# DMA in strict turns from the fourth pair on: a pair's loads, its transposes, then the next pair's loads, held back on POOL

## The chip, the core and the metric

One core of one Trainium2 chip runs the kernel. The metric is the device time of one execution in microseconds (us). The profile of one execution is a little shorter than its device time: 207.6 us of span against 209.35 us for the kernel before. Lower is better. The engines are named as in the profile: PE is TensorE's matmuls, PEld its weight loads, DVE is VectorE, ACT is ScalarE, POOL is GpSimd, SP is SyncE (here it only issues DMAs). L381 is line 381 of that kernel's file; the same line of code has another number in another version.

## The reference

Retention attention with a decaying state per head, then a dense layer with `h * cos(h)` between its two matmuls.

```python
# q, k, v: (4, 8, 768, 64); w_in: (512, 2048); w_out: (2048, 512)
for t in range(S):
    state = gamma * state + outer(k[t], v[t])      # per batch and head
    y[t] = scale * q[t] @ state
x = y.transpose(0, 2, 1, 3).reshape(3072, 512)
h = x @ w_in
out = (h * cos(h)) @ w_out
```

## The kernel before

The sequence is cut into 12 "pairs": pair `p` is one chunk of 128 positions of two batches. For each pair q, k and v are loaded (six loads of 256 KB), from pair 3 on q and v are scaled and converted to bf16 by POOL and k is converted by ACT (the first pairs are shared out otherwise), q and k are transposed (by PE for pairs 0 to 3, by DMA from pair 4 on), and PE computes scores (`stage_a`), outputs and state (`stage_y`). Two pairs give a group of 512 tokens; each group goes through the dense layer. The attention of later pairs is interleaved with the dense layer of earlier groups.

All work of an engine is done in the program's order (in the trace after the change ACT sat idle for 1.8 us at a k conversion, up to 76.1 us, while outputs finished by 72.2 us stood behind it). The program uses seven work banks of 128x512 in PSUM, the memory that matmuls write to; a matmul into a bank must wait until DVE or ACT has read the bank's old content (once for 2.7 us, in the same trace). ACT does both the k conversions, which wait for loads, and the evictions of banks, for which PE waits.

```python
NB = 3                                       # buffers of qk, vs, qkt
SLOT = [0, 1, 2, 3, 2, 4, 0, 1, 3, 2, 4, 0]  # load buffer of each pair

def conv_k(p, on_act):                       # two batches
    for b in range(2):                       # [cut: the branch for DVE]
        nc.scalar.copy(out=qk[p % NB][:, b, 1], in_=kf[SLOT[p]][b])   # ACT
        clk.run("act", 0.6)                  # the build's own model, for picking banks

def stage_t_dma(p):
    for b in range(2):                       # [arguments cut]
        nc.sync.dma_start_transpose(out=qkt[n][:, b]..., in_=qk[n][:, b]...)

# ... after group 0's first layer; [cut]
conv_k(3, True)
conv_q(3, nc.gpsimd)
load(nc.sync, 4, ("q0", "q1"))
load(nc.gpsimd, 4, ("k0", "k1", "v0", "v1"))
conv_v(3, nc.gpsimd)
load(nc.sync, 5, ("q0", "q1", "v0"))
load(nc.gpsimd, 5, ("k0", "k1", "v1"))
# ... [cut]
pair_f(2, 0)
stage_t(3, 0)                                # pair 3 is transposed by PE
stage_t(3, 1)
pair_f(2, 1)
attend(3)
conv_q(4, nc.gpsimd); conv_v(4, nc.gpsimd); conv_k(4, True)
stage_t_dma(4)
load(nc.gpsimd, 6, ("q0", "k0", "q1", "k1", "v0", "v1"))   # two pairs ahead
```

So loads run about two pairs ahead of their use, and nothing keeps a transpose from running beside loads.

## Time and profile before

| | before |
|---|---|
| device time, median of 3 runs | 209.25 us (208.85 to 209.31) |
| span of the profile | 207.6 us |
| PE busy | 96% |
| DVE, ACT, POOL busy | 55%, 55%, 49% |
| granted TensorE clock | 1.0 throughout |

From the profile page of the kernel before: busy time of the engines, then the busy share in tenths in 40 equal slices, and the two lines of the chain of waits that ended last.

```profile
PE 199.5 (96%) x1624; PEld 113.5 (55%) x1646; DVE 113.3 (55%) x188; ACT 114.1 (55%) x193; POOL 102.3 (49%) x118
PE   6889999999999999999999999999999999999993
PEclk9999999999999999999999999999999999999999
PE 91%; DVE 4%; DMA 2%; issue 1%; DVEq 0%
```

PE is full from the fourth slice to the last but one, and 91% of the chain is PE's own work. My reading of this: only less PE work or shorter start and end can help here, and any new PE wait is paid in full (after the change, 5.0 us of waits and 0.9 us less PE work came with a span that is 4.7 us longer).

Next, of the kernel before, the waits of PE and those of ACT for k loads between 40 and 140 us (who waited for whom: us in total, times, longest), and, for the DMA transposes, the time from issue to landing.

```profile
PE bank L381 <- issue: 0.3, 2, 0.2
PE bank L340 <- issue: 0.2, 1, 0.2
ACT qk L210 <- DMA kf<-in_k_dram: 1.0, 1, 1.0
```

```profile
DMA to landing us min/median/max: 2.7/4.6/13.8
```

PE waits for no other engine in these 100 us. ACT waits once for a k load. One transpose took 13.8 us to land, but nobody waited for it.

### The profile page before, as it was taken

Reading aid. Unit: us, or ns where it says so; the run is one execution under the profiler, and the core shown is the slowest. Engines: PE = TensorE matmul, PEld = TensorE weight load, DVE = VectorE, ACT = ScalarE, POOL = GpSimd, SP = SyncE. Lnnn points to the kernel's source line nnn. Section 1 sums busy time; section 2 is a strip of 40 time slices with the busy share of each in tenths; the row PEclk is TensorE's granted clock in tenths of the full one; section 3 lists DMA queues with packets and bytes.
Section 4 is the critical chain, followed back from the end, with each engine's and each line's share of the span. In section 5 each row is a group of like instructions: output and inputs, shape, how many; then the busy total and the mean of one; then the engine's idle time right before and its main releaser. Section 6 shows DMA issues by size and latency. Waiting matters only on the chain.

```text
span 207.6 us, 4155 instructions
## 1 busy us (share of the span) xinstructions
PE 199.5 (96%) x1624; PEld 113.5 (55%) x1646; DVE 113.3 (55%) x188; ACT 114.1 (55%) x193; POOL 102.3 (49%) x118
## 2 busy tenths in 40 slices
PE   6889999999999999999999999999999999999993
PEld 1467554558997555546544465544465444444452
DVE  4691984554957454869874466854367244443000
ACT  6767872257996336577753754653554653553120
POOL 8999238399999999999995230000000000000000
PEclk9999999999999999999999999999999999999999
DMA  6999999999999999959799931141101100110222
GB/s 158 351 237 203 215 252 287 336 261 358 258 251 257 264 252 254 255 184 218 242 177 92 252 82 50 55 103 51 51 3 51 51 18 36 51 52 21 80 77 78
DMA packets 36644, 33.83 MB, mean 163 GB/s; under 512 B 26768, under 2 KB 29072, under 8 KB 36624
## 3 DMA queue, kind: packets, MB, share of 16 engines
q0 software_dynamic: 7808, 20.98, 39.4%
q1 hardware_dynamic: 27632, 12.23, 25.4%
q10 hardware_dynamic: 1184, 0.36, 0.7%
q8 instruction: 13, 0.21, 0.4%
q14 instruction: 7, 0.06, 0.1%
HBM read 27.26 MB, written 6.29 MB: 162 GB/s over the span
## 4 chain that ended last, share of the span: by engine, by line
PE 91%; DVE 4%; DMA 2%; issue 1%; DVEq 0%
PE bank L381 38%; PE bank L340 32%; PE bank L351 7%; PE bank L281 3%; PE bank L259 3%; PE bank L286 2%; DMA qf<-in_q_dram 2%; DVE am L268 2%; PE bank L398 2%; PE bank L232 1%; PE st_ps L303 1%; DVE qk L197 1%; DVE qkt L216 1%; PE bank L362 1%; PE bank L369 1%
## 5 line engine op out<-in xcount | busy, mean ns | idle before, releaser
L333 DVE TENSOR_TENSOR gt<-bank,cosb 128x512 bf16<-128x512 f32 x96 | 64.9, 689 | 61.9 <-ACT cosb L329 61.4
L329 ACT ACTIVATE cosb<-bank,halfpi 128x512 bf16<-128x512 f32 x96 | 65.1, 688 | 50.0 <-PE bank L340 44.4
L381 PE MATMUL bank<-w_out_sb,gt 128*128 128x512 bf16 x359 | 88.5, 379 | 0.7 <-issue 0.3
L340 PE MATMUL bank<-xt,w_in 128*128 128x512 bf16 x294 | 74.3, 380 | 0.7 <-issue 0.3
L381 PEld LDWEIGHTS <-gt 128*128 128x128 bf16 x368 | 35.5, 98 | 41.2
L340 PEld LDWEIGHTS <-w_in 128*128 128x128 bf16 x304 | 33.7, 114 | 30.9
L268 DVE TENSOR_TENSOR am<-bank,mask 128x512 bf16<-128x512 f32 x48 | 30.4, 682 | 3.9 <-PE bank L259 3.9
L388 ACT COPY ob<-bank 128x512 f32<-128x512 f32 x23 | 13.4, 586 | 18.4 <-PE bank L381 18.4
L204 POOL TENSOR_TENSOR vs<-vf,gk 128x512 bf16<-128x512 f32 x21 | 21.4, 1045 | 2.9 <-PE st_ps L303 2.9
L132 POOL DMA_DIRECT2D vf<-in_v_dram x23 | 20.3, 885 | 4.8 <-DMA w_out_sb<-in_moe_w_out_dram 4.8
L197 POOL TENSOR_TENSOR qk<-qf,gq 128x512 bf16<-128x512 f32 x18 | 18.5, 1051 | 7.8 <-issue 4.9
L132 POOL DMA_DIRECT2D kf<-in_k_dram x21 | 18.9, 901 | 1.8 <-DMA w_out_sb<-in_moe_w_out_dram 1.6
L210 ACT CAST qk<-kf 128x512 bf16<-128x512 f32 x24 | 13.9, 615 | 9.3 <-DMA kf<-in_k_dram 9.3
L290 ACT CAST xt<-bank 128x512 bf16<-128x512 f32 x24 | 12.9, 589 | 6.7 <-PE bank L286 6.7
L132 POOL DMA_DIRECT2D qf<-in_q_dram x18 | 16.2, 902 | 0.8 <-DMA w_in<-in_moe_w_in_dram 0.8
L351 PE MATMUL bank<-xt,w_in 128*128 128x256 bf16 x128 | 14.7, 273 | 0.0
L351 PEld LDWEIGHTS <-w_in 128*128 128x128 bf16 x128 | 13.8, 114 | 0.4
L286 PE MATMUL bank<-am,vs 128*64 128x128 bf16 x192 | 11.6, 220 | 0.0
L281 PEld LDWEIGHTS <-stb 128*64 128x64 bf16 x160 | 8.7, 109 | 4.3 <-issue 3.8
L281 PE MATMUL bank<-qkt,stb 128*64 128x128 bf16 x160 | 10.7, 222 | 0.3 <-DVE am L268 0.3
L286 PEld LDWEIGHTS <-vs 128*64 128x64 bf16 x192 | 9.9, 110 | 0.5 <-issue 0.4
L315 DVE CAST stb<-st_ps 64x512 bf16<-64x512 f32 x12 | 8.2, 685 | 2.7 <-PE st_ps L303 2.6
(46 smaller groups left out, 86.8 us busy)
## 6 DMA issues: line engine op xcount, KB each, us to landing
vf<-in_v_dram POOLq DMA_DIRECT2D x23, 256.0 KB, 5.8
out_dram<-ob SPq DMA_DIRECT2D x23, 256.0 KB, 2.0
kf<-in_k_dram POOLq DMA_DIRECT2D x21, 256.0 KB, 5.7
qf<-in_q_dram POOLq DMA_DIRECT2D x18, 256.0 KB, 5.3
w_out_sb<-in_moe_w_out_dram POOLq DMA_DIRECT2D x4, 512.0 KB, 12.5
qf<-in_q_dram SPq DMA_DIRECT2D x6, 256.0 KB, 8.1
w_in<-in_moe_w_in_dram POOLq DMA_DIRECT2D x3, 512.0 KB, 8.1
kf<-in_k_dram POOLq DMA_DIRECT2D x1, 512.0 KB, 5.4
```

What stands on the lines that cost most here:

```text
L132: eng.dma_start(out=t[SLOT[p]][b], in_=src[2 * bp + b, :, ds(c * C, C)].rearrange("h t d -> t h d"))
L197: eng.tensor_tensor(out=qk[p % NB][:, b, 0], in0=qf[SLOT[p]][b], in1=bc(gq, p % NC), op=ALU.mult)
L204: eng.tensor_tensor(out=vs[p % NB][:, b], in0=vf[SLOT[p]][b], in1=bc(gk, p % NC), op=ALU.mult)
L210: nc.scalar.copy(out=qk[p % NB][:, b, 1], in_=kf[SLOT[p]][b])
L268: nc.vector.tensor_tensor(out=am[p % 2][b][j], in0=ap[j], in1=mask.unsqueeze(1).to_broadcast([128, HP, 128]), op=ALU.mult)
L281: nc.tensor.matmul(yp[ts(j, 64), a, :], lhsT=stb[p % 2][:, b, a, ts(j, 64)], rhs=qt(n, b, a), start=True, stop=False, skip_group_check=True)
L286: nc.tensor.matmul(yp[ts(j, 64), a, :], lhsT=vs[n][:, b, 2 * a + j, :], rhs=am[p % 2][b][j][:, a, :], start=(c == 0), stop=True, skip_grou ...
L329: nc.scalar.activation(out=cb, in_=bank, func=AF.Sin, bias=halfpi)
L333: nc.vector.tensor_tensor(out=out, in0=bank, in1=cb, op=ALU.mult)
L340: nc.tensor.matmul(bank, lhsT=w_in_t(i, f), rhs=xt[g % 2][:, i, :], start=(i == 0), stop=(i == KIN - 1))
L351: nc.tensor.matmul(bank[:, ts(e, 256)], lhsT=w_in_t(i, f + e), rhs=xt[g % 2][:, i, ts(hf, 256)], start=(i == 0 and e == 0), stop=(i == KIN ...
L381: nc.tensor.matmul(bank, lhsT=gt[g % 2][:, f, ts(j, 128)], rhs=w_out_sb[:, f, :], start=(f == 0), stop=(f == KOUT - 1))
```

## The change

The intent is to keep transposes and loads apart. A pair's transposes are issued when its loads are in and converted; the next pair's loads are held back until the first of these transposes has landed. The hold is a tiny POOL copy (`gate`) that reads the last columns of the first transpose's result; POOL issues the loads, so they cannot overtake it (in the trace after the change a gate starts at 58.40 us and takes 0.18 us, and the next load's issue starts at 58.86). Pair 3 is transposed by DMA too. k conversions and transposes get new places in the schedule. The diff is shown in excerpts.

```diff
+    gate = sb([128, 2], BF16, "gate")
 ...
-    conv_k(3, True)
-    conv_q(3, nc.gpsimd)
-    load(nc.sync, 4, ("q0", "q1"))
-    load(nc.gpsimd, 4, ("k0", "k1", "v0", "v1"))
-    conv_v(3, nc.gpsimd)
-    load(nc.sync, 5, ("q0", "q1", "v0"))
-    load(nc.gpsimd, 5, ("k0", "k1", "v1"))
+    def fetch(p):
+        load(nc.gpsimd, p, ("k0", "q0", "k1", "q1", "v0", "v1"))
+
+    def turn(p):
+        conv_q(p, nc.gpsimd)
+        stage_t_dma(p)
+        conv_v(p, nc.gpsimd)
+        if p + 1 < NP:
+            nc.gpsimd.tensor_copy(out=gate, in_=qkt[p % NB][:, 0, 1, HP - 1, 126:])
+            fetch(p + 1)
+
+    turn(3)
 ...
-    stage_t(3, 0)
-    stage_t(3, 1)
     pair_f(2, 1)
+    conv_k(4, True)
     attend(3)
-    [conv_q, conv_v, conv_k, stage_t_dma of 4, load of 6]
+    turn(4)
 ...
     pair_f(3, 0)
+    pair_f(3, 1)
     conv_k(5, True)
-    stage_t_dma(5)
-    pair_f(3, 1)
+    turn(5)
     pair_f(3, 2)
     pair_f(3, 3)
 ...
     o_units(1, 2, 6)
-    later(4)
+    conv_k(6, True)
+    stage_y(4)
     attend(5)
+    turn(6)
     o_units(1, 6, 10)
 ...
+    k_at = {(2, 3): 7, (2, 9): 8, (3, 1): 9, (3, 7): 10, (3, 12): 11}   # conv_k at (group, step)
+    t_at = {(2, 4): 7, (2, 10): 8, (3, 2): 9, (3, 8): 10, (3, 13): 11}  # turn
```

The places of scores and outputs in PE's order stay as they were.

More of the change, by code (lines that the diff above doesn't have):

```diff
@@ L493 @@
             conv_v(2, nc.vector, (1,))
+            conv_k(3, True)
         elif u == 11:
             stage_m(2, stage_a(2, 1))
-    conv_k(3, True)
-    conv_q(3, nc.gpsimd)
-    load(nc.sync, 4, ("q0", "q1"))
-    load(nc.gpsimd, 4, ("k0", "k1", "v0", "v1"))
-    conv_v(3, nc.gpsimd)
-    load(nc.sync, 5, ("q0", "q1", "v0"))
-    load(nc.gpsimd, 5, ("k0", "k1", "v1"))
+    def fetch(p):
[8 more added lines that the diff above has]
+    turn(3)
     for j in range(4):
@@ L507 @@
     pair_f(2, 0)
-    stage_t(3, 0)
-    stage_t(3, 1)
     pair_f(2, 1)
+    conv_k(4, True)
     attend(3)
-    conv_q(4, nc.gpsimd)
-    conv_v(4, nc.gpsimd)
-    conv_k(4, True)
-    stage_t_dma(4)
-    load(nc.gpsimd, 6, ("q0", "k0", "q1", "k1", "v0", "v1"))
+    turn(4)
     pair_f(2, 2)
@@ L520 @@
     pair_f(2, 3, (1,))
-    conv_q(5, nc.gpsimd)
-    conv_v(5, nc.gpsimd)
-    load(nc.gpsimd, 7, ("q0", "k0", "q1", "k1", "v0", "v1"))
     pair_f(3, 0)
+    pair_f(3, 1)
     conv_k(5, True)
-    stage_t_dma(5)
-    pair_f(3, 1)
+    turn(5)
     pair_f(3, 2)
-    conv_q(6, nc.gpsimd)
-    conv_k(6, True)
-    conv_v(6, nc.gpsimd)
     pair_f(3, 3)
-    def ahead(p):
-        if p < NP:
-            conv_q(p, nc.gpsimd)
-            conv_k(p, True)
-            conv_v(p, nc.gpsimd)
-    def fetch(p):
-        load(nc.gpsimd, p, ("q0", "k0", "q1", "k1", "v0", "v1"))
-    def later(p):
-        stage_y(p)
-        n = 8 if p == 4 else p + 3 if p > 5 else NP
-        if n < NP:
-            fetch(n)
     late = []
@@ L568 @@
     attend(4)
-    stage_t_dma(6)
     o_units(1, 2, 6)
-    later(4)
+    conv_k(6, True)
+    stage_y(4)
     attend(5)
+    turn(6)
     o_units(1, 6, 10)
-    later(5)
+    stage_y(5)
+    k_at = {(2, 3): 7, (2, 9): 8, (3, 1): 9, (3, 7): 10, (3, 12): 11}
+    t_at = {(2, 4): 7, (2, 10): 8, (3, 2): 9, (3, 8): 10, (3, 13): 11}
+    a_at = {(2, 2): 6, (2, 10): 7, (3, 2): 8}
+    y_at = {(2, 6): 6, (2, 14): 7, (4, 14): 11}
     for g in range(2, NG + 1):
         for s in range(16):
-            hf, r = divmod(s, 8)
-            p = 2 * (g + 1) + hf
             if g == 2 and s % 2 == 0 and s < 12:
@@ L588 @@
                     last_o(g - 1, 3)
-            while late and late[0][0] <= 16 * g + s:
+            now = 16 * g + s
+            while late and late[0][0] <= now:
                 late.pop(0)[1]()
-            if p < NP:
-                if r == 0:
-                    ahead(p + 1)
-                elif r == 1:
-                    if p + 1 < NP:
-                        stage_t_dma(p + 1)
-                elif r == 2 and p in (6, 7, 8):
-                    todo = [stage_a(p, b) for b in range(2)]
-                    stage_m(p, todo[0])
-                    put_off(16 * g + s + 1, lambda todo=todo, p=p: stage_m(p, todo[1]))
-                elif r == 6 and p in (6, 7, 11):
-                    later(p)
-                elif (g, s) == (3, 4):
-                    fetch(11)
-                if (g, s) in joined:
-                    join(joined[g, s], 16 * g + s)
+            at = (g, s)
+            if at in k_at:
+                conv_k(k_at[at], True)
+            if at in t_at:
+                turn(t_at[at])
+            if at in a_at:
+                p = a_at[at]
+                todo = [stage_a(p, b) for b in range(2)]
+                stage_m(p, todo[0])
+                put_off(now + 1, lambda todo=todo, p=p: stage_m(p, todo[1]))
+            if at in y_at:
+                stage_y(y_at[at])
+            if at in joined:
+                join(joined[at], now)
 _INS = ['q', 'k', 'v', 'moe_w_in', 'moe_w_out']
```

## The prediction

> **What bounds the kernel.** TensorE. The page's busy table has PE at 96% of a 207.6 us span, granted clock 1.0 in all slices. One-microsecond windows show it between 0.95 and 1.00 almost everywhere from 28 us on. After 17 us the chain of waits is a row of matmuls back to back: one unit of four 128x512 matmuls takes 0.86 us, followed at once by the next. DVE, ACT (55% each) and POOL (49%) have slack on average. DMA does not bound the time, although it looks ugly: issue times and landings in the trace show transposes of one pair landing in 2.7 to 3.2 us when alone (pairs 6 and 11) and in 8.2 and 13.8 us when six loads are in flight (pair 9, issued at 102 us). [...] But nobody waits for those late landings: in the table of waits the only PE waits for qkt are on DVE copies early on.
>
> **What the change does.**
> - Removes the 16 PE transposes of pair 3: 0.89 us of the chain of waits (at 49.39 us), all on the critical path. Also two DVE copies of 0.68 us, off it.
> - Adds one DMA transpose pair and nine tiny POOL copies as gates [...]. Off the path.
> - Moves loads: the loads of pair p+1 start when the first transpose of pair p has landed. Transposes should now land in about 3 to 4 us each.
>
> **Does the serial chain meet its deadlines?** Estimate of one turn from the trace's durations: a POOL load issue takes 0.88 us and lands about 4.0 us after its start when little else runs, so from a turn's start the second k lands at 5.8 us, the second q at 6.7, the last v at 8.4. POOL: issues to 5.3, first q conversion (1.05 us) to 6.4, second to 7.8, the two v conversions to 9.8. First transpose from 6.4 to about 9.6. So a turn takes about 10 to 11.5 us. With pair 4's loads starting at 44 to 45 us, the transposes of pairs 4 to 8 land near 57, 67, 77, 88 and 98 us; PE wants them at about 65.5, 71, 80.5, 92.5 and 104. Slack is 3 us or more. The tight spot is ACT, which runs in order: its k conversions of pairs 6, 8 and 9 sit in front of evictions and wait for their loads, by my estimate up to 2 us for pair 6 (near 70 us) and under 1 us elsewhere. Seven PSUM banks should hide most of this. I allow 0.1 to 0.3 us of new PE waits.
>
> **Predicted.** 209.25 - 0.89 + about 0.15 = 208.5 us; 8 in 10 between 207.9 and 210.2. Chances: faster by over 2% 0.01, within 2% 0.93, slower by over 2% 0.06.
>
> **What would show it right or wrong.** Right: PE busy about 198.6 us; 16 fewer PE transposes; the chain still all matmuls after 17 us; transpose landings under about 5 us; total DMA bytes equal but the loads spread to about 125 us; ACT waits for k loads near 70 us. Wrong: PE waits at the first score matmuls of pairs 5 or 6 (for a qkt DMA), or PE waits for banks that an ACT blocked behind a k conversion holds.
>
> **What would make it wrong.** A turn longer than 12 us (transposes still collide with the last v loads): the delay adds up turn by turn, and PE would lose several microseconds between 70 and 105 us.

## The result, and the profile after

| | before | after |
|---|---|---|
| device time, median of 6 runs | 208.91 us (208.85 to 209.31) | 214.50 us (214.11 to 219.68) |
| ratio of the fast runs | | 1.0278 (95%: 1.0232 to 1.0325) |
| span of the profile | 207.6 us | 212.3 us |

Ratios here and below are the mean time of one kernel's fast runs over that of the kernel before in the same rounds, so not quite the ratio of the medians. The change made the kernel slower by 2.8%. One of its six runs (219.68 us) was slow and is left out of the ratio; a run is labelled slow when it is over 1.5% above the fastest of the same kernel.

The same lines of the page after the change:

```profile
PE 199.0 (94%) x1608; PEld 112.6 (53%) x1630; DVE 111.4 (52%) x186; ACT 114.5 (54%) x193; POOL 108.4 (51%) x131
PE   6889999999997949998899999999999999999993
PE 63%; DMA 16%; POOL 9%; issue 5%; DVE 4%; ACT 2%; POOLq 0%; DVEq 0%; ACTq 0%; SPq 0%
```

PE's instructions fell by 16, as planned. But PE's row now has holes between the 13th slice and the 20th (64 to 106 us), and the chain is PE's own work for 63% only; DMA and POOL have come into it.

Waits after the change, of PE, then of ACT for k loads, between 40 and 140 us, and the landing of the transposes:

```profile
PE bank L382 <- ACT xt L291: 2.7, 1, 2.7
PE bank L260 <- DVE gt L334: 1.4, 2, 1.0
PE bank L287 <- DVE am L269: 0.4, 1, 0.4
PE bank L341 <- DVE gt L334: 0.3, 1, 0.3
PE bank L341 <- ACT ob L389: 0.3, 1, 0.3
ACT qk L211 <- DMA kf<-in_k_dram: 14.8, 9, 3.8
```

```profile
DMA to landing us min/median/max: 2.7/3.5/6.3
```

PE now waits 5.0 us (the rounded lines add up to 5.1): 4.6 us for a *bank* that DVE or ACT has not read yet, 0.4 us for masked scores (`am`) of DVE, and never for a transpose. With 0.9 us of PE transposes gone this accounts for 4.1 of the 4.7 us by which the span grew; PE also waited 0.4 us more before 20 us, where the change does nothing. The transposes land faster than before. The other new number is ACT's: 14.8 us of waiting for k loads, 1.0 before. The time order of ACT and PE shows how the two are tied. First ACT after the change, 62 to 77 us (start, duration, what, and in brackets its idle time before and what ended it), then PE.

```profile
62.48 0.62 ACT L211 CAST qk<-kf 128x512 bf16<-128x512 f32 x1 [1.89 <-DMA kf<-in_k_dram]
64.45 0.62 ACT L211 CAST qk<-kf 128x512 bf16<-128x512 f32 x1 [1.35 <-DMA kf<-in_k_dram]
64.98 2.42 ACT L330 ACTIVATE cosb<-bank,halfpi 128x512 bf16<-128x512 f32 x4
69.28 0.59 ACT L389 COPY ob<-bank 128x512 f32<-128x512 f32 x1 [1.89 <-PE bank L382]
73.70 0.62 ACT L211 CAST qk<-kf 128x512 bf16<-128x512 f32 x1 [3.83 <-DMA kf<-in_k_dram]
76.13 0.62 ACT L211 CAST qk<-kf 128x512 bf16<-128x512 f32 x1 [1.81 <-DMA kf<-in_k_dram]
76.65 1.07 ACT L291 CAST xt<-bank 128x512 bf16<-128x512 f32 x2
```

```profile
65.02 0.40 PE L260 MATMUL bank<-qkt 64*128 64x128 bf16 x8
66.44 0.21 PE L260 MATMUL bank<-qkt 64*128 64x128 bf16 x1 [1.02 <-DVE gt L334]
67.03 0.38 PE L260 MATMUL bank<-qkt 64*128 64x128 bf16 x7 [0.38 <-DVE gt L334]
...
72.95 1.67 PE L382 MATMUL bank<-w_out_sb,gt 128*128 128x512 bf16 x7 [0.16 <-issue]
77.28 1.89 PE L382 MATMUL bank<-w_out_sb,gt 128*128 128x512 bf16 x8 [2.66 <-ACT xt L291]
```

Read the second tie first. PE had finished pair 4's outputs by 72.2 us, and ACT had been idle since 69.9. But the next instruction in ACT's order was pair 6's k conversion (L211), whose loads landed at 73.7 and 76.1 us. Only at 76.65 could ACT copy out pair 4's outputs (`xt`), and PE got a bank at 77.28. In the first tie ACT's cosines stand behind pair 5's k conversions; DVE needs the cosine to empty the bank, and PE needs the bank.

Why are the loads late? POOL after the change, one whole turn:

```profile
58.40 0.18 POOL L506 COPY gate<-qkt 128x2 bf16<-128x2 bf16 x1 [1.03 <-DMA qkt<-qk]
58.86 0.92 POOL L133 DMA_DIRECT2D kf<-in_k_dram  x1 [0.28 <-issue]
...
61.54 0.88 POOL L133 DMA_DIRECT2D qf<-in_q_dram  x1
62.41 1.76 POOL L133 DMA_DIRECT2D vf<-in_v_dram  x2
64.18 1.05 POOL L198 TENSOR_TENSOR qk<-qf,gq 128x512 bf16<-128x512 f32 x1
66.33 1.04 POOL L198 TENSOR_TENSOR qk<-qf,gq 128x512 bf16<-128x512 f32 x1 [1.09 <-DMA qf<-in_q_dram]
67.33 2.04 POOL L205 TENSOR_TENSOR vs<-vf,gk 128x512 bf16<-128x512 f32 x2
69.32 0.18 POOL L506 COPY gate<-qkt 128x2 bf16<-128x2 bf16 x1
```

Six issues (5.3 us), a wait for the second q, two q and two v conversions: 10.6 us from one turn's first load to the next, and nothing in it can overlap with another turn. The seven turns from pair 4 to pair 11 took 13.9, 10.6, 10.6, 11.2, 12.3, 10.4 and 11.5 us, 11.5 on average. The gate at the end of this turn waited for nothing; only in three of eight turns did POOL wait there for the transpose, 1.0 us (the first line above), 0.4 and 0.2 us.

### The profile page after: what moved, and what is told of

Read it like the earlier page. It is cut to its first block, busy times and chain, and to the rows that moved or that the text cites. A ratio compares the mean times of both kernels' runs of the same rounds, so it can differ in the third digit from the quotient of the medians.

```text
span 212.3 us, 4131 instructions
## 1 busy us (share of the span) xinstructions
PE 199.0 (94%) x1608; PEld 112.6 (53%) x1630; DVE 111.4 (52%) x186; ACT 114.5 (54%) x193; POOL 108.4 (51%) x131
## 4 chain that ended last, share of the span: by engine, by line
PE 63%; DMA 16%; POOL 9%; issue 5%; DVE 4%; ACT 2%; POOLq 0%; DVEq 0%; ACTq 0%; SPq 0%
PE bank L382 29%; PE bank L341 23%; DMA qf<-in_q_dram 7%; DMA kf<-in_k_dram 4%; POOL kf L133 3%; DMA qkt<-qk 3%; DMA vf<-in_v_dram 3%; POOL qf L133 2%; DVE am L269 2%; PE bank L399 2%; PE bank L352 2%; PE bank L282 1%; PE bank L287 1%; POOL vs L205 1%; PE bank L260 1%
## 5 line engine op out<-in xcount | busy, mean ns | idle before, releaser
L334 DVE TENSOR_TENSOR gt<-bank,cosb 128x512 bf16<-128x512 f32 x96 | 64.8, 689 | 71.3 <-ACT cosb L330 70.9
L341 PE MATMUL bank<-xt,w_in 128*128 128x512 bf16 x294 | 74.6, 380 | 1.3 <-issue 0.4
L211 ACT CAST qk<-kf 128x512 bf16<-128x512 f32 x24 | 14.5, 616 | 23.7 <-DMA kf<-in_k_dram 23.7
L198 POOL TENSOR_TENSOR qk<-qf,gq 128x512 bf16<-128x512 f32 x18 | 19.0, 1054 | 13.7 <-DMA qf<-in_q_dram 11.4
L133 POOL DMA_DIRECT2D vf<-in_v_dram x24 | 21.1, 884 | 5.2 <-DMA w_out_sb<-in_moe_w_out_dram 5.2
L133 POOL DMA_DIRECT2D qf<-in_q_dram x22 | 19.5, 887 | 0.8 <-DMA w_in<-in_moe_w_in_dram 0.8
L352 PEld LDWEIGHTS <-w_in 128*128 128x128 bf16 x128 | 13.8, 114 | 0.4
L260 PE MATMUL bank<-qkt 64*128 64x128 bf16 x192 | 8.5, 218 | 2.7 <-DVE gt L334 1.4
L282 PE MATMUL bank<-qkt,stb 128*64 128x128 bf16 x160 | 10.8, 223 | 0.3 <-DVE am L269 0.3
## 6 DMA issues: line engine op xcount, KB each, us to landing
w_out_sb<-in_moe_w_out_dram POOLq DMA_DIRECT2D x4, 512.0 KB, 12.9
```

What stands on the lines that cost most here:

```text
L133: eng.dma_start(out=t[SLOT[p]][b], in_=src[2 * bp + b, :, ds(c * C, C)].rearrange("h t d -> t h d"))
L198: eng.tensor_tensor(out=qk[p % NB][:, b, 0], in0=qf[SLOT[p]][b], in1=bc(gq, p % NC), op=ALU.mult)
L282: nc.tensor.matmul(yp[ts(j, 64), a, :], lhsT=stb[p % 2][:, b, a, ts(j, 64)], rhs=qt(n, b, a), start=True, stop=False, skip_group_check=True)
L334: nc.vector.tensor_tensor(out=out, in0=bank, in1=cb, op=ALU.mult)
L341: nc.tensor.matmul(bank, lhsT=w_in_t(i, f), rhs=xt[g % 2][:, i, :], start=(i == 0), stop=(i == KIN - 1))
L352: nc.tensor.matmul(bank[:, ts(e, 256)], lhsT=w_in_t(i, f + e), rhs=xt[g % 2][:, i, ts(hf, 256)], start=(i == 0 and e == 0), stop=(i == KIN ...
```

## The experiments

My theory (A) after the result: PE loses time only through ACT's order, k conversion before eviction. Rivals: (B) the chain of load, conversion and transpose is slower than PE wants, so that PE is dragged by it wherever ACT's instructions stand; (C) the gate, the strictness as such, costs. In all experiments on the changed kernel but e12, PE's and DVE's instructions and banks are identical with the changed kernel's (compared in the built programs; the calls of the build's own clock model were left where they were, so that it picks the same banks; the diffs are shortened), so only what is named differs.

The second k load of each pair landed, or ACT first wanted k, at these times (us; from the traces' landing times and ACT's timeline; in e8 ACT never waits for these loads, so it shows when ACT would come to its k conversion):

| pair | 5 | 6 | 7 | 8 | 9 | 10 | 11 |
|---|---|---|---|---|---|---|---|
| ACT wants k (e8) | 60.5 | 68.0 | 85.1 | 93.8 | 104.8 | 116.6 | 126.4 |
| second k landed, changed kernel | 64.4 | 76.1 | 86.1 | 97.2 | 109.5 | 119.7 | 132.1 |
| second k landed, e13 | 63.4 | 72.6 | 83.4 | 92.3 | 103.1 | 114.4 | 124.3 |

By e8, ACT wants a new k every 11 us on average, but pair 6's only 7.5 us after pair 5's, which is shorter than any turn of the changed kernel. The largest lateness arises there, and not from the average pace alone.

### e1 and e2: move one k conversion behind the evictions

```diff
-    conv_k(6, True)
     stage_y(4)
+    conv_k(6, True)      # e1
```
```diff
-    conv_k(5, True)
-    turn(5)
     pair_f(3, 2)
     pair_f(3, 3)
+    conv_k(5, True)      # e2
+    turn(5)
```

> Only ACT's order changes: the two k conversions of pair 6 come after, not before, the two evictions of pair 4's outputs. PE's and DVE's instructions and the PSUM banks stay as they are, and the loads arrive as late as in the changed kernel (second k of pair 6 near 76 us). My theory (A): PE loses time because in-order ACT sits at a k conversion whose load is late, while finished PSUM banks behind it are not evicted. Then the 2.66 us PE wait at 74.6 us goes away almost whole; some may come back at the next k conversion (pair 7, which ACT reaches near 84 us, 2 us before its load), so 211.5 to 213.0 us against 214.5. Rival (B): PE is late because transposes, or data for the score matmuls, are late; then nothing in the time changes: 214.2 to 214.8. Rival (C): the slower pace of the DMA itself slows all: also no change.

> Only ACT's order changes: the k conversions of pair 5 come after the cosines of that pair group's last four evictions, not before. Theory A: the 1.42 us of PE waits at 65.5 to 67 us (score matmuls of pair 4 that wait for banks, not for transposes) goes away; PE then comes to pair 6's wait 1.4 us earlier, while the loads of pair 6 are no earlier, so that wait may grow by up to the same 1.4 us: 213.0 to 214.5 us, and in the profile the wait at 66 us is gone and the one near 74 us is 2.7 to 4.1 us. Rival B (late transposes): the wait at 66 us stays.

Measured: e1 215.64 us (ratio 1.0334, 1.0308 to 1.036), e2 215.70 us (1.0304, 1.0248 to 1.036). In both the targeted wait went, as A says. In both the time did not fall, and both lie above the ranges I expected (e2's wait near 74 us, 3.4 us, was as forecast). The longest wait of PE in e1, and e1's windows around the long one (window, length, busy of PE, PEld, DVE, ACT, POOL with instruction counts, granted clock, DMA share, GB/s):

```profile
PE bank L349 <- ACT ob L397: 4.2, 1, 4.2
```

```profile
95.00:99.00 4.00, 0.00 (x0) 0.00 (x0) 0.00 (x0) 1.61 (x3) 3.01 (x5) 0.95 0.93 281
99.00:102.00 3.00, 2.84 (x7) 1.02 (x7) 2.27 (x4) 1.96 (x4) 2.86 (x3) 0.50 0.74 208
102.00:106.00 4.00, 4.00 (x61) 2.51 (x60) 3.99 (x8) 2.73 (x5) 3.29 (x5) 1.00 0.59 142
```

The 2.7 us wait at 74.6 us has become one of 4.2 us at 95 us, behind pair 8's k conversion: PE came earlier, the loads did not. And a second cost shows: the granted clock was 0.5 for 3.41 us, from 98.6 to 102.0 us. PE worked in 2.84 us of this, seven matmuls in all; in the changed kernel's trace, at a clock of 1.0, a row of seven 128x512 matmuls took 1.67 us. At a clock of 0.5 about half of the 2.84 us is lost, 1.4 us (an estimate from this time and the clock), and 1.7 us if PE works through all of the 3.41 us. Not every wait is followed by this: e4 (waits of 2.1 and 0.4 us; clock 0.85 and 0.81 in the two windows of 5 us from 70 us on) and e5 (one of 3.0 us; mean clock 0.992 over the run) had it, while the profiled run of the changed kernel (2.7 us) kept a clock of 1.00, and e2's (3.4 us) has a mean clock of 0.997, against 0.992 in e1. What starts it, these runs do not show. The two longest runs of the changed kernel have mean clocks of 0.976 and 0.984, though one at 0.992 took 214.40 us, no longer than the rest.

### e3: all k conversions later on ACT, with their turns

```diff
-    t_at = {(2, 4): 7, (2, 10): 8, (3, 2): 9, (3, 8): 10, (3, 13): 11}
+    t_at = {(2, 5): 7, (2, 12): 8, (3, 5): 9, (3, 11): 10, (4, 1): 11}   # conv_k just before turn
      # [cut] and both moves of e1 and e2
```

> Both moves above, and the k conversions of pairs 7 to 11 two to four steps later on ACT (pair 7 at step 5 of group 2, 8 at step 12, 9 at step 5 of group 3, 10 at step 11, 11 at step 1 of group 4), so that ACT comes to each about when its load has landed. PE's and DVE's order and banks unchanged, loads and gate unchanged. Theory A: nearly all 5.9 us of new PE waits go; what stays is that transposes of pairs 5 and 6 land up to 0.5 us after PE wants them: 208.3 to 209.5 us. If the load chain itself (a turn of 11.4 us on average) is what PE must keep up with, as rival B has it, PE waits move to the score matmuls and the time stays above 212.

Measured: 212.25 us (210.41 to 214.32; ratio 1.0128, 1.0075 to 1.0182). Better than the changed kernel, but not the 208.3 to 209.5 I expected. Its profile (which fell in a slow run) has 4.1 us of PE waits, behind the same kind of conversion of pairs 6 and 8: the places were still too early for these loads.

The sums of PE waits longer than 0.2 us after 20 us, in the profiles, are: changed kernel 5.0, e1 4.6, e2 5.6, e3 4.1. Moving one k conversion (e1, e2) moves the wait and saves no time. Moving all of them (e3) takes back over half of the loss in the fast runs (a ratio of 1.0128, not 1.0278), and its 4.1 us, from a slow run, cannot speak against that. So ACT's order matters, as A says, but A does not explain all: the loads themselves come late.

### e8: ACT never waits for k

```diff
-                nc.scalar.copy(out=qk[p % NB][:, b, 1], in_=kf[SLOT[p]][b])
+                nc.scalar.copy(out=qk[p % NB][:, b, 1],
+                               in_=kf[SLOT[p] if p < 4 else 2 if p == 7 else 1][b])   # wrong data
```

> Wrong result on purpose: in the changed kernel ACT converts, from pair 4 on, k tiles of a pair that landed long ago, so ACT never waits for a k load. Loads, their order, gate, q and v conversions, transposes, PE, DVE stay. If PE is dragged only through ACT's waits (bank evictions behind a k conversion), the PE waits of 5 us fall to under 1 us and the time is 208.5 to 209.8 us, clock 1.0. If the serial chain of loads, conversions and transposes is too slow for PE whatever ACT does, PE waits for transposes appear instead (score matmuls of pairs 5 to 8), 2 us or more, and the time stays over 211 us.

Measured: 210.58 us (208.40 to 212.16; ratio 1.0041, 0.9979 to 1.0103); result wrong on purpose. PE's waits now, 38 us on, other than its own issue:

```profile
PE bank L260 <- DMA qkt<-qk: 2.4, 4, 0.7
```

All waits for banks are gone; most of the loss, 2.4 of 2.8% by the ratios of the fast runs, went through ACT. What is left is a wait for transposes of pairs 5 and 6 at 70 to 72 and 81 to 83 us: about what B says. So both are true: one late chain, and two ways in which it reaches PE, the larger one through ACT.

### e5: no gate; e11: no gate and e1's move

```diff
         conv_v(p, nc.gpsimd)
         if p + 1 < NP:
-            nc.gpsimd.tensor_copy(out=gate, in_=qkt[p % NB][:, 0, 1, HP - 1, 126:])
             fetch(p + 1)
```

> The changed kernel with the POOL gate copies taken out, so that a pair's loads are issued as soon as POOL has done the conversions of the pair before. In the changed kernel's trace POOL waits for the transpose at only three of eight gates (1.0, 0.4 and 0.2 us); everywhere else the v conversions end later than the transpose. My reading: what makes the turns serial is POOL's own order (next loads behind this pair's conversions, which wait for this pair's loads), not the gate: by pair 6 the loads are about 1.5 us earlier, the second transposes run beside them, PE waits fall by at most 1.5 us: 212.5 to 214.5 us. Rival: the gate, the strict turn, is what costs: then most of the 5.6 us comes back, under 210.5 us.

> No gate, and pair 6's k conversions behind pair 4's evictions on ACT: the no-gate run had one PE wait alone, 3.0 us behind this k conversion, and one spell of 3.4 us at half clock (1.7 us) just after it. If this wait goes without coming back: 208.3 to 209.5 us. If PE then meets the next late load (pair 7 or 8, by my estimate 1 to 2.4 us after ACT wants it), as in the run with the same move under the gate: 210 to 213 us.

Measured: e5 213.03 us (ratio 1.016, 1.0107 to 1.0212), e11 215.34 us (1.0304, 1.0286 to 1.0321). Without the gate a turn is 10.8 us on average, not 11.5, and about 2.4 us come back (1.2% between the ratios), somewhat more than I allowed. By the ratios more than half of the loss stays (the verdict against the kernel before is "unclear", with 1.1 to 2.1% of loss): the serial order is in POOL's program, not only in the gate. So C is a part of the cause, not all of it. e11 lies above both ranges I had given: PE met the wait again at 94.5 us (4.1 us) and the half clock after it, as in e1 (mean clock 0.990).

### e6: output stores out of the way of the longest turn

```diff
-            nc.sync.dma_start(out=dst, in_=o)
+            if g == 0: held.append((dst, o))
+            else: nc.sync.dma_start(out=dst, in_=o)
 ...
     turn(4)
+    for dst, o in held: nc.sync.dma_start(out=dst, in_=o)
```

> The four output stores of the first group are issued behind the transposes of pair 4, not before them, so that they are not in flight beside pair 4's loads and first transpose (in the changed kernel these loads land in 4.6 to 6.6 us and that transpose in 6.3 us, and turn 4 takes 13.9 us, against 10.5 to 10.6 us in the two turns after it). My reading: the longest turn is long because of these stores. Then turn 4 takes about 11.5 us, loads of pairs 5 and 6 land 2 to 2.5 us earlier, and PE waits fall from about 5 to about 2.5 to 3 us: 211 to 212.5 us. Rival: the load chain is slow by itself: turn 4 stays at 13 us or more and the time at 214 to 215 us.

Measured: 214.42 us (ratio 1.0245, 1.0209 to 1.028): no clear gain. The turn of pair 4 did shorten, from 13.9 to 10.7 us, so the four stores are why it was long. But the stores then ran beside pair 5's loads, whose second k took 7.1 us to land, and that turn took 12.9 us, not 10.6. The average stayed 11.5 us. Here the DMA work that was moved met the next pair's loads.

### e12: pair 3 back on PE

```diff
-        stage_t_dma(p)
+        if p > 3: stage_t_dma(p)      # and the gate for p > 3 only
 ...
     pair_f(2, 0)
+    stage_t(3, 0)
+    stage_t(3, 1)
     pair_f(2, 1)
```

> The changed kernel with pair 3 transposed on PE as before: 0.89 us of PE work put back, loads and turns otherwise as they are (no gate for pair 3, where POOL did not wait for it). If PE is paced by the load chain from pair 5 on, this work fills time that PE would wait anyway: no change, 214.0 to 215.2 us, and the first PE waits near 66 us shorter by about the same 0.9 us. If the chain of waits is still PE's own work, it adds 0.9 us: 215.4 us.

Measured: 215.37 us (214.68 to 217.09; ratio 1.0321, 1.0275 to 1.0368). Inconclusive: the interval overlaps that of the changed kernel, and 0.9 us cannot be told from the runs' own spread. In its profile the score matmuls (L260) wait 1.5 us in all for banks behind DVE's `gt`, 1.4 in the changed kernel's.

### e4 and e9: strict gate, but loads two pairs ahead

```diff
             nc.gpsimd.tensor_copy(out=gate, ...)
-            fetch(p + 1)
+            for n in (4, 5) if p == 3 else (p + 2,) if p + 2 < NP else ():
+                fetch(n)                                # e4
```
```diff
     # e9: as e4, and for p > 3 the next pair's q conversion stands before the gate
+        conv_q(p + 1, nc.gpsimd)
         nc.gpsimd.tensor_copy(out=gate, ...)
         fetch(p + 2)
```

> The changed kernel with its gate, but loads go two pairs ahead: the first gate releases the loads of pairs 4 and 5, and each later turn those of the pair after next. ACT's order is as in the changed kernel. Theory A: k loads have landed long before ACT comes to them, ACT waits for k only at pair 4, and the saving of 0.89 us shows: 208.0 to 209.0 us. If instead the strict gate (loads held until the first transpose has landed) is what costs, this version, which has the same gate, stays above 212.

> A try at a version that beats both: loads two pairs ahead, and on POOL the q conversions of the next pair are put before the gate and the next loads, so that transposes can be issued as soon as ACT's k conversion is done. The earlier two-ahead run had one PE wait alone, 2.5 us for pair 5's transpose, whose q conversion stood behind six load issues on POOL; here that transpose is issued near 62 us, not 68.6, and should land by 67 us, before PE wants it at about 70. If late loads and late q conversions were all that was wrong: no PE wait after 40 us, clock 1.0, 208.0 to 208.6 us. If transposes issued beside loads are what costs: they now run beside the loads of the pair after next, land in 6 us or more, and the time is over 211 us, or over 240 as in the run with pair 3 by DMA in the kernel before.

Measured: e4 214.40 us (ratio 1.0264, 1.0223 to 1.0304), which missed the 208.0 to 209.0 that theory A had forecast, e9 209.40 us (208.88 to 212.43; 1.0005, 0.9985 to 1.0025). In e4's profile no bank wait is left; pair 5's transpose came late (its q conversion stood behind six load issues), PE waited 2.5 us and then ran 3.41 us at half clock. e9 mends that and is level with the kernel before. What it does not show is the saving: PE waits 1.0 us for pair 8's second transpose, which took 10.3 us to land beside loads. This is the meeting that strict turns were meant to prevent. In e4 the device time was 2.9 us longer than the span of its profile, in the other profiled runs 1.7 to 2.5 (up to 3.0 in single runs of other kernels too, as in the slow run of the changed kernel); that I cannot explain.

### e7 and e10: one part of the change alone, in the kernel before

```diff
     conv_q(3, nc.gpsimd)
+    stage_t_dma(3)                      # e7
     load(nc.sync, 4, ("q0", "q1"))
 ...
     load(nc.sync, 5, ("q0", "q1", "v0"))
+    stage_t_dma(3)                      # e10: here, not above
 ...
-    stage_t(3, 0)
-    stage_t(3, 1)
```

> The kernel before with one part of the change alone: pair 3 is transposed by DMA, not by PE; loads as before, no gate. If the 0.89 us of PE transposes was worth what the prediction said, and its transposes land before PE wants them at about 51 us though loads run beside them, then 208.0 to 208.3 us (ratio 0.996 to 0.998), no new PE wait and a granted clock of 1.0 in all runs. If transposes beside loads are what had to be avoided, PE waits for pair 3 near 51 us and the time rises over 209.

> The kernel before with pair 3 transposed by DMA again, but these transposes stand behind all loads of pairs 4 and 5 on SP, not before most of them. In the first try they pushed SP's loads and stores back, pair 4's transpose was issued at 58.3 us, not 53.3, and from there on transposes landed in 12 to 29 us beside loads in 16 to 23 us. If that delay on SP's queue started the breakdown: here loads are on time, pair 4's transpose near 53 us, and the time is 208 to 210 us (pair 3's transposes may land at 50 to 52 us, a little late). If two more transposes among the loads are too many whatever their place: over 215 us again.

Measured: e7 246.56 us (253.25, 212.26, 249.71, 243.41), e10 239.68 us (235.34 to 262.22). Both fell under the worse of the two cases I had named (over 209 us, over 215 us), and far beyond its bound. The waits of PE in e7, the landing of its transposes, and two of its windows:

```profile
PE bank L259 <- DMA qkt<-qk: 35.7, 7, 10.4
```

```profile
DMA to landing us min/median/max: 2.7/10.9/29.4
```

```profile
70.00:80.00 10.00, 4.24 (x24) 1.86 (x25) 3.77 (x6) 1.24 (x3) 6.59 (x7) 0.50 1.24 120
90.00:100.00 10.00, 0.00 (x0) 0.00 (x0) 1.27 (x2) 0.00 (x0) 6.49 (x8) 0.50 1.30 76
```

(The columns are those of e1's windows.) The DMA engines are busy all the time (share 1.24 and 1.30) and move 120 and 76 GB/s; the kernel before moved 261 and 201 in the same windows. Transposes and loads in flight together were both slower (at the median from issue to landing, transposes 10.9 us against 4.6 in the kernel before, k loads issued by POOL 12.1 against 5.7), and PE waited for the transposes of pairs 4 to 7. One run of e7 in four (212.26 us) escaped most of it. The kernel before has 16 such transposes, one of which took 13.8 us, and was steady in all its runs; two more were enough to tip it, whether pair 3's transposes stood before SP's loads or behind them. Both profiles fell in runs labelled slow, and e7's runs gave no ratio; e10's fast runs alone are at 1.1283 (1.1261 to 1.1306). In e7 the clock fell only after PE had waited (1.00 from 40 to 65 us, 0.84 from 65 to 70, where PE was busy for 0.53 us, and 0.50 from 70 to 80), so the waits for transposes are the cause and not the clock. What in the DMA engines makes the meeting so dear, no run here shows; it stays open.

### e13, e14 and e15: a shorter turn

```diff
     def turn(p):
         conv_q(p, nc.gpsimd)
         stage_t_dma(p)
+        if p + 1 < NP:
+            load(nc.sync, p + 1, ("q0", "q1"))
         conv_v(p, nc.gpsimd)
         ...
     def fetch(p):
-        load(nc.gpsimd, p, ("k0", "q0", "k1", "q1", "v0", "v1"))
+        load(nc.gpsimd, p, ("k0", "k1", "v0", "v1"))
```

> The changed kernel, strict turns and gate and ACT order as they are, but the next pair's two q loads are issued by SP, right behind this pair's transposes, so that POOL issues four loads per turn and not six (3.5 us, not 5.3). The second k then lands about 5 us after a turn's start, not 5.8 to 6.9, the first q conversion starts about 1.3 us earlier, and a turn is about 9 to 10 us (estimate from the issue, landing and conversion times of the changed kernel), not 11.4. If the length of the turn against PE's pace of about 10 us per pair is what costs, PE waits after 60 us fall from 5 us to 2 us or less, clock 1.0, 208.3 to 211 us. If what costs is the gate or any waiting of loads for transposes as such, 213 us or more.

> As the run before, with pair 6's k conversions behind pair 4's evictions on ACT. Under the long turns this move only shifted the wait from 74 to 95 us. With turns shorter than PE's pace the later pairs' loads are early enough, so the wait should now go for good: 208.0 to 209.5 us. If it comes back near 95 us, turns are still too long: 210 to 213 us.

> The two-ahead version with early q conversions (209.4 us, one PE wait of 1.0 us for pair 8's second transpose, which landed 10.3 us after its issue beside loads), with q loads issued by SP behind the transposes. If the shorter POOL turn lets transposes be issued before the loads that they met: no PE wait, 208.0 to 208.6 us, the saving of 0.9 us shown. If transposes and loads still meet on SP and POOL together: landings of 6 to 10 us or the breakdown with over 220 us.

Measured: e13 209.32 us (208.67 to 210.07; ratio 1.0019, 0.9994 to 1.0045), e14 209.56 us (208.85 to 211.21; 1.0051, 1.0 to 1.0102), e15 214.50 us (210.72 to 217.61). PE's waits in e13, 38 us on, then a turn of POOL, then the landing of its transposes:

```profile
PE bank L260 <- DVE gt L334: 0.4, 1, 0.4
PE bank L382 <- ACT xt L291: 0.3, 1, 0.3
```

```profile
58.34 1.80 POOL L133 DMA_DIRECT2D kf<-in_k_dram  x2 [0.30 <-issue]
60.13 1.77 POOL L133 DMA_DIRECT2D vf<-in_v_dram  x2
61.91 2.05 POOL L198 TENSOR_TENSOR qk<-qf,gq 128x512 bf16<-128x512 f32 x2
64.25 2.04 POOL L205 TENSOR_TENSOR vs<-vf,gk 128x512 bf16<-128x512 f32 x2 [0.29 <-DMA vf<-in_v_dram]
66.33 0.19 POOL L508 COPY gate<-qkt 128x2 bf16<-128x2 bf16 x1
66.86 1.80 POOL L133 DMA_DIRECT2D kf<-in_k_dram  x2 [0.34 <-issue]
```

```profile
DMA to landing us min/median/max: 2.7/2.8/5.7
```

The strict order and the gate are kept, ACT's order is kept, the transposes land in 2.8 us at the median, and the loss is gone. This turn took 8.5 us, where the same turn of the changed kernel took 10.6; over the seven turns e13's mean is 10.5 us, not the 9 to 10 that I expected, against 11.5. In the table above the loads of pairs 7 to 11 are now in before ACT comes to them, and those of pairs 5 and 6 at most 4.6 us late (e8's own times from pair 7 on contain its 2.4 us of PE waits). SP's issue of the two q loads mostly took 1.2 us in all. The shorter turn is not all: with q on SP the second k is also issued second on POOL, not third. e5 began pair 6's loads at 67.2 us, only 0.4 us after e13, but its second k landed at 74.8 us, e13's at 72.6. The changed kernel with its k loads first and all six on POOL was not tried, so what is shown is that earlier k loads under strict turns remove the loss, and not how much of it the order of the loads gives. In e14 the move of pair 6's conversion no longer comes back as a wait (0.7 us in its profile), as expected, but the time is no better. Three of e15's four runs are labelled slow, so it has no ratio; its profile, of a slow run, had one PE wait of 5.9 us for pair 5's second transpose, which landed 12.3 us after its issue beside two pairs' loads, and the clock was then 0.5 for 6.8 us: the meeting of transposes and loads is back.

No version beat the kernel before beyond the noise. The 16 transposes are gone from PE in e13 too, but 0.6 us of PE waits stay, and its spans (206.8 to 207.4 us in four runs, 207.1 to 207.3 for the kernel before on the same chip) do not show the saving of 0.9 us.

## Why the prediction was wrong

- **PE is the bound, and transposes of pair 3 are 0.89 us of it.** As far as shown, right: PE has 16 instructions fewer. e13's span less its remaining PE waits is 207.4 - 0.6 = 206.8 us, 0.8 below the profile of the kernel before, but only 0.3 to 0.5 below that kernel's spans on e13's chip, so the size of the saving in time is not shown.
- **Transposes land in under about 5 us.** Mostly right: median 3.5 us, but 6.3 us in the turn of pair 4.
- **"A turn takes about 10 to 11.5 us."** At the edge: 11.5 on average, but 13.9 for the first, because four output stores ran beside its loads (e6). The transposes forecast near 57 and 67 us for pairs 4 and 5 landed (the second of each) at 59.3 and 71.3.
- **The step that failed: "Seven PSUM banks should hide most of this. I allow 0.1 to 0.3 us of new PE waits."** I had the mechanism (ACT in order, k conversions in front of evictions) and the place (pair 6, near 70 us), but with "up to 2 us for pair 6 ... and under 1 us elsewhere". ACT waited 3.2 us at pair 5 and 5.6 us at pair 6, and PE 5.0 us in all. The prediction's own list of signs had named this, as what would show it wrong: "PE waits for banks that an ACT blocked behind a k conversion holds". The banks do hide some: in e13 ACT waits of 2.1 us (pair 5) and 3.1 us (pair 6) reached PE as 0.4 and 0.3 us; in the changed kernel 3.2 and 5.6 us reached it as 1.4 and 2.7. A hidden margin of two to three us was treated as if it covered anything.
- **Why the deadline check passed.** I checked when transposes are wanted by PE, where I counted 3 us to spare (in e8 they were not there: PE waited 2.4 us for transposes of pairs 5 and 6), and not when k is wanted by ACT. ACT wanted pair 6's k at 68.0 us (e8); it came at 76.1. By the prediction's own numbers (a start at 44 to 45 us, two turns of 10 to 11.5 us, 5.8 us to the second k) it would have come at 70 to 74 us, up to 6 us too late; I called that 2 us.
- **Not in the prediction at all:** after a PE wait the clock was 0.5 for 3.41 us in e1 and in e4, up to 1.7 us more (an estimate: half of the 3.41 us). The two longest runs of the changed kernel have mean clocks of 0.976 and 0.984; its profiled run had 1.0.
- **"What would make it wrong"** named the right consequence (PE waits between 70 and 105 us) with a threshold, 12 us per turn, that was too lenient.

## What to carry to other kernels

When DMA is made serial, compute the length of one full turn (issue, landing, conversion, transpose) and compare it with the pace of *every* consumer, the earliest first, and with the shortest time between two of its demands (7.5 us here), not only the mean; here that was not PE but a conversion that shares an in-order engine with PSUM evictions. If moving an instruction makes a wait vanish at one place and come back later with the same sum, stop moving and shorten the chain: here two of six load issues were taken off the busy issuing engine, which also brought the second k forward. A schedule that runs transposes beside loads may be fine and one small step from collapse (here 208.9 us, and 246.6 us with two more transposes, e7), so test such a part of a change alone.
